# The last batch of a capacity-limited expert layer: exact rank counts against a frozen top-80 list in place of sorting, with the late weights loaded into dead attention tiles

## The chip, the cores and the metric

One core of a Trainium2 chip runs the whole program. The metric is device microseconds of one execution. Engines are named as in the profile: PE (TensorE, matmuls; PEld its weight loads), DVE (VectorE), ACT (ScalarE), POOL (GpSimd), SP (SyncE); the text uses the long names. SP issues most DMAs, POOL those of the expert weights, the gathers and the scatters.

## What is computed

Chunked sparse attention for 4 batches of 8 heads (768 tokens, 64 wide), then a mixture of 8 experts over the 3072 tokens of the attention's result (512 wide), in which each expert keeps only its 80 tokens of highest gate value:

```python
# attention, per batch and head: each query row sees its 6 best key chunks of 32 (by an upper bound), causally
scores = where(selected & causal, scale * q @ k.T, -1e9);  x = softmax(scores) @ v      # x: (3072, 512)
logits = x @ w_gate                                  # (3072, 8)
expert_idx = argmax(logits, axis=1);  gate_w = softmax(logits)[arange(N), expert_idx]
for e in range(8):
    tok_idx = where(expert_idx == e)[0]
    if len(tok_idx) > 80:
        tok_idx = tok_idx[argpartition(-gate_w[tok_idx], 80)[:80]]     # the 80 largest
    out[tok_idx] = gate_w[tok_idx, None] * (relu(x[tok_idx] @ w1[e]) @ w2[e])
```

All other rows of `out` are zero.

## The kernel before

The attention works on 8 quads of 4 heads; batch b has quads 2b and 2b+1. A quad is 6 rounds of four score steps: one round for its first 256 query rows (t = 0), two for t = 1, three for t = 2. So there are 48 rounds, numbered 0 to 47, and the loop over `rd` writes the work of all of them in one order. Inside `manual_schedule` that order is what TensorE and SyncE execute; for VectorE, ScalarE and GpSimd the scheduler fixes an order when the program is compiled, and each of these engines then executes its list strictly in that order.

One block (g, t) passes through these stages. `score` (L338) makes score matmuls, ScalarE their exponentials E (L349), and GpSimd masks the blocks on the diagonal (L352). One round later `value` (L357) and `denom` (L369) multiply E, masked, with V and with ones. After the block's last round `evacuate` (L387) copies the numerators; two rounds after it `gate_rows` (L392) adds the gate logits to the denominators and VectorE copies the result to `DSB` (L400); three rounds after it `scales` (L403) transposes DSB, takes reciprocals and, for the second quad of a batch, runs `gates` (L443), whose chain of small VectorE operations goes from `den` (L412) to `gmask` (L473): per token and expert the gate value, or -1 where the token has another expert. Four rounds after it `rows` (L427) transposes the numerators, scales them to x and stores them in `x_dram`. Meanwhile `prep` (L216) makes the next quad's K and Q (`kf`, `kmm` L235 and L237, `qp` L260), its chunk bounds (`bound`), their ranks (`rank`) and the copies of the result into QX (`unselect`, L309 and L312).

`merge` (L481) keeps the sorted 80 best gate values of each expert. TensorE transposes `gmask` to `ps_g` (8 partitions), ScalarE copies it behind the list (L487), and VectorE makes 10 MAX8 (L493) and 9 MATCH_REPLACE8 (L495) passes over 80 + 128 n values:

```python
for r in range(CAP // 8):
    nc.vector.max(out=top, in_=src[:, 0:w])
    if r < CAP // 8 - 1:
        nc.vector.match_replace(out=src[:, 0:w], in_to_replace=top, in_values=src[:, 0:w], imm_value=-2.0)
        yield
```

Batches 0 to 2 are merged at 848 wide each (the merge of batch 2 begins in round 38), batch 3 in three merges of 336 at up to four steps a round, the rest of them after the loop. Only then come the threshold `tau`, `picks`, the scan, the counts `ps_cum`, `slot`, 24 selections `sel` (L643) with 24 index matmuls (L645), and `gidx` (L651): which token sits in slot s of expert e. GpSimd gathers those rows of x with eight indirect DMAs (L656), and each expert's MLP runs (L665 and L689). The weights of experts 0 to 4 are loaded during the attention. Those of experts 5 to 7, six DMAs of 1 MB (L126, L132), go into a pool that is opened after the attention's pools are closed.

## Time and profile before

| | us |
|---|---|
| median of 3 runs (lowest, highest) | 380.48 (379.87, 381.7) |
| the profiled execution | 381.24 |
| its span, first to last instruction | 379.5 |
| mean granted TensorE clock in it | 0.902 of full speed |
| busy: PE, DVE, ACT, POOL | 291.0 (77%), 247.0 (65%), 161.8 (43%), 157.9 (42%) |

The span is what the rows below are times of: microseconds from its start. A granted clock of 1.0 is 2.4 GHz, 0.5 is 1.2 GHz. "Idle before <- releaser" in a row is how long the engine stood before it and which engine's work ended that.

### The profile page before, as it was taken

What the parts mean: (1) busy time and instruction counts of PE and PEld (TensorE: products, weight loads), DVE (VectorE), ACT (ScalarE), POOL (GpSimd) and SP (SyncE); (2) the same over time, 40 slices, a digit from 0 to 9 for tenths busy, and PEclk for the clock granted to TensorE, in tenths of its full rate; (3) what the DMA queues carried; (4) which work ended last, traced back from release to release, by engine and by line L of the source; (5) the groups of instructions that cost most, each with busy time, mean ns of one, the idle gap of its engine ahead of it and who ended that gap; (6) DMA issues with size and microseconds to landing.
All of it is one profiled execution on the core that took longest, in us unless ns stands there. A gap on an engine that the chain in (4) does not pass through costs nothing. (4 is left out here: it accounts for less than half of the span.)

```text
span 379.5 us, 9779 instructions
## 1 busy us (share of the span) xinstructions
PE 291.0 (77%) x3860; PEld 192.3 (51%) x3860; DVE 247.0 (65%) x808; ACT 161.8 (43%) x353; POOL 157.9 (42%) x360
## 2 busy tenths in 40 slices
PE   2639999999987989998978999898995303118882
PEld 1316667666644755674555667454763102116560
DVE  7684155556699856678996566799588898202331
ACT  2327548547644644764456368535550000002220
POOL 7878407816810762493047319402120050521221
PEclk9986999999999899999989999999996655557998
DMA  9972505998997499999909965000000079990110
GB/s 176 201 124 51 118 3 100 186 259 212 197 256 160 84 145 200 270 202 234 234 11 175 200 117 115 30 0 3 3 29 29 28 124 200 208 202 15 38 53 28
DMA packets 95805, 47.63 MB, mean 126 GB/s; under 512 B 76710, under 2 KB 88102, under 8 KB 95760
## 3 DMA queue, kind: packets, MB, share of 16 engines
q1 hardware_dynamic: 82320, 28.35, 34.1%
q0 software_dynamic: 13440, 18.67, 28.7%
q8 instruction: 30, 0.49, 0.6%
q14 instruction: 15, 0.12, 0.1%
HBM read 53.10 MB, written 10.76 MB: 168 GB/s over the span
## 5 line engine op out<-in xcount | busy, mean ns | idle before, releaser
L349 ACT ACTIVATE E<-ps_S 128x512 f32<-128x512 f32 x192 | 89.4, 550 | 61.1 <-PE ps_S L346 61.1
L364 PE MATMUL ps_num<-E,vn 128*32 128x256 f32 (+1 forms) x1536 | 94.2, 363 | 0.0
L352 POOL TENSOR_SCALAR_AFFINE_SELECT E<-E 128x256 f32<-128x256 f32 x96 | 37.2, 414 | 107.9 <-ACT E L349 106.7
L364 PEld LDWEIGHTS ps_num<-E,vn 128*32 128x32 f32 x1536 | 51.9, 112 | 31.6 <-issue 2.5
L383 PE MATMUL ps_den<-E,ones 128*32 128x256 f32 (+1 forms) x768 | 51.7, 359 | 4.6 <-DVE DSB L400 4.6
L493 DVE MAX8 cand<-cand 8x8 f32<-8x848 f32 (+1 forms) x60 | 45.8, 763 | 9.2 <-ACT cand L487 8.4
L346 PE MATMUL ps_S<-QX,KX 128*128 128x256 bf16 (+1 forms) x384 | 47.7, 267 | 4.3 <-ACT QX L312 2.3
L241 POOL CAST KX<-kf 64x384 bf16<-64x384 f32 x64 | 32.8, 513 | 26.8 <-ACT kf L231 24.6
L346 PEld LDWEIGHTS <-KX 128*128 128x128 bf16 x384 | 37.1, 100 | 10.5 <-issue 5.3
L495 DVE MATCH_REPLACE8 cand<-cand,cand 8x848 f32<-8x848 f32 (+1 forms) x54 | 40.4, 748 | 0.1
L383 PEld LDWEIGHTS ps_den<-E,ones 128*32 128x32 f32 x768 | 26.3, 111 | 16.5 <-DVE DSB L400 5.9
L227 PE MATMUL ps_k<-ident_f,kn 128*128 128x128 f32 x96 | 19.2, 317 | 9.4 <-DMA kn<-in_k_dram 4.8
L235 DVE TENSOR_REDUCE kmm<-kf 128x12 f32<-128x384 f32 x32 | 17.5, 546 | 12.5 <-ACT kf L231 12.2
L434 DVE TENSOR_TENSOR x_nat<-ps_xn,rec 128x512 bf16<-128x512 f32 x24 | 16.3, 680 | 10.8 <-PE ps_xn L433 10.7
L389 ACT ACTIVATE npt<-ps_num 128x512 f32<-128x512 f32 x24 | 14.3, 597 | 19.1 <-PE ps_num L364 19.1
L231 ACT ACTIVATE kf<-ps_k 128x384 f32<-128x384 f32 x32 | 16.2, 507 | 14.1 <-PE ps_k L227 8.2
L672 ACT ACTIVATE XT<-ps_XT 128x320 bf16<-128x320 bf16 x8 | 3.5, 436 | 42.2 <-PE ps_XT L669 42.2
L254 PE MATMUL ps_q<-ident_f,qn 128*128 128x128 f32 x96 | 19.0, 314 | 2.8 <-DMA qn<-in_q_dram 2.7
L682 DVE TENSOR_SCALAR HT<-ps_H 128x320 bf16<-128x320 f32 x8 | 3.9, 492 | 24.9 <-PE ps_H L679 24.9
L257 ACT ACTIVATE qf<-ps_q 128x384 f32<-128x384 f32 x32 | 16.5, 516 | 8.3 <-PE ps_q L254 8.1
L698 POOL DMA_INDIRECT out_dram<-Y,sidx x8 | 7.4, 922 | 28.2 <-DVE Y L696 25.8
L260 DVE TENSOR_SCALAR qp<-qf 128x256 f32<-128x256 f32 (+1 forms) x32 | 13.1, 411 | 8.4 <-ACT qf L257 8.4
(118 smaller groups left out, 448.5 us busy)
## 6 DMA issues: line engine op xcount, KB each, us to landing
w<-in_moe_w_dram POOLq DMA_DIRECT2D x16, 1024.0 KB, 12.7
kn<-in_k_dram SPq DMA_DIRECT2D x32, 192.0 KB, 4.0
qn<-in_q_dram SPq DMA_DIRECT2D x32, 192.0 KB, 4.7
vn<-in_v_dram SPq DMA_DIRECT2D x32, 192.0 KB, 3.7
out_dram<-zero_tile SPq DMA_DIRECT2D x12, 512.0 KB, 11.1
x_dram<-x_nat SPq DMA_DIRECT2D x12, 257.0 KB, 4.3
X<-x_dram,gidx POOLq DMA_INDIRECT x8, 6.9
out_dram<-Y,sidx POOLq DMA_INDIRECT x8, 2.6
```

Source lines behind the costliest of these rows:

```text
L227: nc.tensor.transpose(ps_k[:, j * P:(j + 1) * P], kn[:, 3 * hf + j, 2 * a:2 * a + 2, :].rearrange("p h d -> p (h d)"), ident_f32[:])
L235: nc.vector.tensor_reduce(out=kmm[a][:, 0, ch], in_=kv, axis=mybir.AxisListType.X, op=ALU.min)
L241: nc.gpsimd.tensor_copy(out=KX[s][2 * a + i][rows, cols], in_=kf[rows, :])
L254: nc.tensor.transpose(ps_q[:, j * P:(j + 1) * P], qn[:, 3 * hf + j, 2 * a:2 * a + 2, :].rearrange("p h d -> p (h d)"), ident_f32[:])
L257: nc.scalar.activation(out=qf[a][:, cols], in_=ps_q[:], func=mybir.ActivationFunctionType.Copy)
L346: nc.tensor.matmul(out=ps_S[:, r, 0:wid], lhsT=KX[s][h][:, kb * P:(kb + 1) * P], rhs=QX[s][h][:, c0:c0 + wid], start=True, stop=True)
L349: nc.scalar.activation(out=E[:, :, 0:wid], in_=ps_S[:, :, 0:wid], func=mybir.ActivationFunctionType.Exp, scale=scale)
L352: nc.gpsimd.affine_select(out=E[:, :, 0:P], in_=E[:, :, 0:P], compare_op=ALU.is_ge, fill=0.0, base=0, pattern=[[0, 2], [1, P]], channel_mu ...
L364: nc.tensor.matmul(out=NUM[q0:q0 + 32, a, c0:THIRD], lhsT=nats[(g, "vn")][:, kb, 2 * a + r, 32 * f:32 * (f + 1)], rhs=Es[st][:, r, 0:wid], ...
L383: nc.tensor.matmul(out=dn[q0:q0 + 32, c0:THIRD], lhsT=ones32[:, a, :], rhs=Es[st][:, r, 0:wid], start=first, stop=False, skip_group_check= ...
L493: nc.vector.max(out=top, in_=src[:, 0:w])
L495: nc.vector.match_replace(out=src[:, 0:w], in_to_replace=top, in_values=src[:, 0:w], imm_value=-2.0)
```

## The change

Batch 2 is no longer merged whole: its first four blocks of 128 tokens are merged at 592 wide as soon as their gates are there (rounds 35 to 38, three steps a round), its last two at 336 (rounds 38 to 41). Batch 3 is not merged at all. In round 42 the list is frozen, and `freeze` spreads over rounds 42 to 47 what stood after the loop: threshold, picks, scan, counts and slots, for the tokens of batches 0 to 2 (18 blocks instead of 24), and beside it each frozen entry's rank.

A token of batch 3 then gets its place by counting: `spread` multiplies the one-hot row of its expert (three bfloat16 parts of the gate value, so that the difference is exact) with the `lists` of the frozen values and of the new tokens, which gives all differences at once; VectorE (`own`, `count`) and ScalarE (`signs`) count how many are positive by accumulating along the row. A place below 80 is the slot that a displaced old entry leaves. Three steps, `turn_new(t)` and `weigh0` to `weigh2`, treat the three thirds of the batch, the last after the loop. The three parts of the gate come from six more operations in `gates`.

The six late weights are loaded as 18 pieces by GpSimd in rounds 40 to 44, into tiles whose last use is over (the K and Q loads, `kf`, `qf`, `qp`, the zero tile, QX and KX of the other set, the V of quad 6). GpSimd also sets up a few constants more at the start.

```diff
-    def load_w1(e, pool):
...
-    def load_w2(e, pool):
...
+    def load_parts(e, which, spaces):
...
+            tc.keep_in_program_order(nc.gpsimd.dma_start(out=dst, in_=src[:, c0:c0 + n, :]))
...
+        def late_weights(rd):
+            if rd == 40:
+                load_parts(5, 0, [bf(nats[(7, "kn")][:]), bf(zt[:])])
+            elif rd == 41:
+                load_parts(5, 1, [bf(nats[(7, "qn")][:]), bf(spare["kf0"]), bf(spare["kf1"])])
+            elif rd == 42:
+                four = [bf(spare[n]) for n in ("qf0", "qf1", "qp0", "qp1")]
+                load_parts(6, 0, [x[:, 0:DFF] for x in four])
+                load_parts(6, 1, [x[:, DFF:DFF + DMOD] for x in four])
+            elif rd == 43:
+                load_parts(7, 0, [bf(QXT[0][:])])
+                load_parts(7, 1, [bf(KXT[0][:]), bf(spare["ubS"])])
+            elif rd == 44:
+                vspace = bf(nats[(6, "vn")][:])
+                load_parts(6, 1, [vspace[:, 0:4 * DMOD]])
+                load_parts(7, 0, [vspace[:, 4 * DMOD:6 * DMOD]])
...
+        def spread(dst, c, span):
+            nc.tensor.matmul(out=dst, lhsT=lists[:, WIDE + P * c:WIDE + P * (c + 1)],
+                             rhs=lists[:, span], start=True, stop=True)
+        def own(view, c, c_lo, acc):
...
+            nc.vector.scalar_tensor_tensor(out=junk[:, 0:n], in0=view, scalar=1.0,
+                                           in1=ties[:, x0:x0 + n], op0=ALU.mult, op1=ALU.is_gt,
+                                           accum_out=acc[:, c:c + 1])
+        def signs(view, c, op, acc):
...
+            nc.scalar.activation(out=junk2[:, 0:n], in_=view, scale=2.0 ** 40,
+                                 bias=(1.0 if op is ALU.is_ge else minus1[:, 0:1]),
+                                 func=mybir.ActivationFunctionType.Sign, accum_out=acc[:, c:c + 1])
...
-            for rd in range(N + 5):
+            for rd in range(N + 1):
...
+                late_weights(rd)
...
+                if rd == FREEZE:
...
+                    fz = freeze(stages)
+                if rd >= FREEZE:
+                    next(fz, None)
+                if rd == N - 1:
+                    turn_new(0)
+                    weigh0()
...
-                    if gi == 1 and (b == NB - 1 or et == 2):
-                        n = 2 if b == NB - 1 else QBLK
-                        merges.append(merge(stages, QBLK * b + 2 * et - n + 2, n))
+                    if gi == 1 and b < NB - 2 and et == 2:
+                        merges.append(merge(stages, QBLK * b, QBLK))
+                    elif gi == 1 and b == NB - 2 and et > 0:
+                        c0, n = ((0, 4), (4, 2))[et - 1]
+                        merges.append(merge(stages, QBLK * b + c0, n))
-                if merges and rd < N:
-                    for _ in range(4 if g == NQUAD - 1 else 2):
+                if merges:
+                    for _ in range(3 if stages > 2 else 2):
...
+            last = ends[N - 1]
+            gate_rows(*last)
+            turn_new(1)
+            scales(*last)
+            weigh1()
+            rows(*last)
+            turn_new(2)
+            weigh2()
...
-        for c in range(TBLK):
-            nc.vector.tensor_scalar(out=sel[:, c, :], in0=slot1[:], scalar1=slot[:, c:c + 1],
-                                    scalar2=None, op0=ALU.is_equal)
-            nc.tensor.matmul(out=ps_idx[:].rearrange("s k e -> s (k e)"), lhsT=sel[:, c, :],
-                             rhs=slotrhs[:, c].rearrange("p k e -> p (k e)"),
-                             start=(c == 0), stop=(c == TBLK - 1))
+            nc.vector.tensor_tensor(out=sel, in0=rooms,
+                                    in1=place[:, :, None].to_broadcast([P, NEWB, CAP]),
+                                    op=ALU.is_equal)
+            for c in range(NEWB):
+                nc.tensor.matmul(out=ps_idx[:].rearrange("s k e -> s (k e)"), lhsT=sel[:, c, :],
+                                 rhs=slotrhs[:, OLDB + c, 3:5, :].rearrange("p k e -> p (k e)"),
+                                 start=(c == 0), stop=False, skip_group_check=True)
+                nc.tensor.matmul(out=ps_idx[:, 0, :], lhsT=sel[:, c, :],
+                                 rhs=slotrhs[:, OLDB + c, 5, :],
+                                 start=False, stop=(c == NEWB - 1), skip_group_check=True)
```

How it moves instructions shows on three engines. VectorE's list in rounds 36 and 37, up to the `DSB` copy of quad 5's last block, before (L309 is the last copy into QX for quad 6; `kmm` and `qp` are the K reductions and the Q copies of the next quad):

```order
L309 COPY QX_0_2_115<-ps_pen_3603 32x640
L434 TENSOR_TENSOR x_nat_2848<-ps_xn_3646,rec_3555 128x2x256
L235 TENSOR_REDUCE kmm0_3637<-kf_3657 128x12
L237 TENSOR_REDUCE kmm0_3637<-kf_3657 128x12
L235 TENSOR_REDUCE kmm0_3637<-kf_3691 128x12
L237 TENSOR_REDUCE kmm0_3637<-kf_3691 128x12
L260 TENSOR_SCALAR qp0_3641<-qf0_3639 128x256
L260 TENSOR_SCALAR qp0_3641<-qf0_3639 128x384
L235 TENSOR_REDUCE kmm1_3638<-kf_3750 128x12
L237 TENSOR_REDUCE kmm1_3638<-kf_3750 128x12
L400 COPY DSB_3800<-ps_den_189 128x256
```

The same place now, from the middle of the first merge of batch 2 (L551 is MAX8, L553 MATCH_REPLACE8; L272 to L297 are `kmm` and `qp`, L438 is the copy to `DSB`):

```order
L297 TENSOR_SCALAR qp0_3720<-qf0_3718 128x384
L553 MATCH_REPLACE cand_0_134<-cand_1_135,cand_0_134 8x592
L272 TENSOR_REDUCE kmm1_3717<-kf_3835 128x12
L551 MAX cand_1_135<-cand_0_134 8x8
L274 TENSOR_REDUCE kmm1_3717<-kf_3835 128x12
L553 MATCH_REPLACE cand_0_134<-cand_1_135,cand_0_134 8x592
L272 TENSOR_REDUCE kmm1_3717<-kf_3867 128x12
L551 MAX cand_1_135<-cand_0_134 8x8
L274 TENSOR_REDUCE kmm1_3717<-kf_3867 128x12
L553 MATCH_REPLACE cand_0_134<-cand_1_135,cand_0_134 8x592
L297 TENSOR_SCALAR qp1_3721<-qf1_3719 128x256
L438 COPY DSB_3885<-ps_den_187 128x256
```

Between the reductions now stand passes of 592, and the copy comes behind six of each kind.

ScalarE's list at the end of the attention before (`npt` are the numerators, `cand` the transposed gates for the merge, `XT` the first expert's input):

```order
L456 ACTIVATE ex_4527<-sh_4525 128x16
L487 ACTIVATE cand_0_141<-ps_g_4593 8x256
L389 ACTIVATE npt_4632<-ps_num_188 128x512
L456 ACTIVATE ex_4653<-sh_4651 128x16
L487 ACTIVATE cand_1_142<-ps_g_4692 8x256
L672 ACTIVATE XT_4865<-ps_XT_4860 128x320
```

And now (L669 copies the transposed new tokens into `lists`, L702 the rooms; L694 are the `signs`):

```order
L494 ACTIVATE ex_4843<-sh_4841 128x16
L669 ACTIVATE lists_108<-ps_n_4900 27x2x256
L702 ACTIVATE cand_1_135<-ps_rooms_4906 128x160
L694 ACTIVATE PEN_1_127,older_192<-ps_a_4914 128x80
L694 ACTIVATE PEN_1_127,older_192<-ps_a_4916 128x80
L694 ACTIVATE PEN_1_127,signed_191<-ps_a_4914 128x256
L694 ACTIVATE PEN_1_127,signed_191<-ps_a_4916 128x256
L694 ACTIVATE PEN_1_127,signed_191<-ps_l_4921,minus1_98 128x256 x2
L952 ACTIVATE XT_5013<-ps_XT_5008 128x320
```

Two copies for the merge are gone; between the last `ex` and the first `XT` stand two copies and six counts.

GpSimd's list from the end of the attention before (L126 and L132 are the late weights, L656 the gathers):

```order
L475 TENSOR_SCALAR slotrhs_140<-oh_4659,pcol_98 128x2x8
L477 TENSOR_TENSOR slotrhs_140<-oh_4659,ccol_100 128x2x8
L479 CAST slotrhs_140<-oh_4659 128x2x8
L126 DMA w1_5_4761<-in_moe_w1_dram 128x4x1024
L132 DMA w2_5_4763<-in_moe_w2_dram 128x8x512
L126 DMA w1_6_4765<-in_moe_w1_dram 128x4x1024
L132 DMA w2_6_4767<-in_moe_w2_dram 128x8x512
L126 DMA w1_7_4769<-in_moe_w1_dram 128x4x1024
L132 DMA w2_7_4771<-in_moe_w2_dram 128x8x512
L656 DMA X_4840<-x_dram_63,gidx_4838 80x257
```

The first late loads now, in rounds 40 to 42 (L150 loads a piece, named by the tile that it goes into; L390 is the mask of E):

```order
L390 AFFINE_SELECT E_4054<-E_4054 128x2x128
L390 AFFINE_SELECT E_4060<-E_4060 128x2x128
L150 DMA kn_3401<-in_moe_w1_dram 128x3x1024
L150 DMA zero_tile_110<-in_moe_w1_dram 128x1024
L150 DMA qn_3406<-in_moe_w2_dram 128x6x512
L150 DMA kf_3835<-in_moe_w2_dram 128x512
L150 DMA kf_3867<-in_moe_w2_dram 128x512
L390 AFFINE_SELECT E_4224<-E_4224 128x2x128
L390 AFFINE_SELECT E_4230<-E_4230 128x2x128
L150 DMA qf0_3718<-in_moe_w1_dram 128x1024
L150 DMA qf1_3719<-in_moe_w1_dram 128x1024
L150 DMA qp0_3720<-in_moe_w1_dram 128x1024
```

The loads stand between masks of E now, and no load stands ahead of the gathers.

## Rows read from the trace of the kernel before

**Rows 1.** Windows; us, then busy PE, PEld, DVE, ACT, POOL, clock, DMA, GB/s.

```profile
262.00:282.00 20.00, 19.79 (x310) 13.57 (x310) 14.81 (x41) 10.84 (x24) 3.73 (x11) 1.00 0.04 15
282.00:296.30 14.30, 9.74 (x111) 5.17 (x108) 11.27 (x44) 2.96 (x7) 1.43 (x5) 0.76 0.06 20
296.30:324.70 28.40, 6.47 (x36) 4.57 (x36) 25.82 (x95) 0.59 (x2) 5.67 (x9) 0.54 0.76 132
324.70:339.50 14.80, 0.05 (x2) 0.05 (x2) 0.22 (x2) 0.00 (x0) 6.72 (x8) 0.50 1.19 221
339.50:379.50 40.00, 27.99 (x352) 20.28 (x352) 9.91 (x16) 6.89 (x16) 8.02 (x9) 0.88 0.13 37
```

**Rows 2.** Timeline of the last round; start, us, engine, line, what [idle <-releaser].

```profile
282.30 1.93 PE L364 MATMUL ps_num<-E,vn 128*32 128x256 f32 x32
...
289.13 0.59 PE L486 MATMUL ps_g<-ident_f,gmask 128*8 128x128 f32 x2 [4.03 <-DVE gmask L473]
...
290.50 3.22 PE L364 MATMUL ps_num<-E,vn 128*32 128x256 f32 x32
...
295.79 0.42 DVE L400 COPY DSB<-ps_den 128x256 f32<-128x256 f32 x1 [1.77 <-PE ps_den L396]
```

**Rows 3.** Timeline from the last `DSB` to the first MLP matmul.

```profile
304.82 0.85 POOL L126 DMA_DIRECT2D w<-in_moe_w_dram  x1 [2.21 <-DVE cand L493]
...
320.58 3.69 PE L645 MATMUL ps_idx<-slotrhs,sel 128*80 128x24 bf16 x24 [2.06 <-DVE sel L643]
...
324.51 0.16 DVE L651 SCALAR_TENSOR_TENSOR gidx<-idx 80x8 int32<-80x8 f32 x1
325.57 1.03 POOL L656 DMA_INDIRECT X<-x_dram,gidx  x1 [15.72 <-issue]
...
339.24 0.90 POOL L656 DMA_INDIRECT X<-x_dram,gidx  x1 [4.21 <-DMA w<-in_moe_w_dram]
339.45 0.45 PE L669 MATMUL ps_XT<-ident_bf,X 80*128 80x80 bf16 x4 [15.19 <-DMA X<-x_dram,gidx]
...
340.50 2.29 PE L679 MATMUL ps_H<-XT,w 128*128 128x80 bf16 x32 [0.61 <-issue]
```

**Rows 4.** VectorE's groups by shape; busy us, mean ns | idle before <-releaser.

```profile
L493 DVE MAX8 cand<-cand 8x8 f32<-8x848 f32 x30 | 30.9, 1029 | 6.6 <-ACT cand L487 6.4
L495 DVE MATCH_REPLACE8 cand<-cand,cand 8x848 f32<-8x848 f32 x27 | 27.4, 1015 | 0.1
L235 DVE TENSOR_REDUCE kmm<-kf 128x12 f32<-128x384 f32 x32 | 17.5, 546 | 12.5 <-ACT kf L231 12.2
...
L493 DVE MAX8 cand<-cand 8x8 f32<-8x336 f32 x30 | 14.9, 497 | 2.6 <-ACT cand L487 2.1
...
L495 DVE MATCH_REPLACE8 cand<-cand,cand 8x336 f32<-8x336 f32 x27 | 13.0, 480 | 0.0
...
L495 DVE MATCH_VALUE_LOAD cand<-cand,cand 8x8 f32 x54 | 4.0, 74 | 0.6
```

**Rows 5.** Timeline of rounds 37 and 38: `DSB`, `gmask` and TensorE behind each.

```profile
233.52 0.42 DVE L400 COPY DSB<-ps_den 128x256 f32<-128x256 f32 x1 [0.32 <-PE ps_den L396]
...
234.42 0.39 PE L383 MATMUL ps_den<-E,ones 128*32 128x256 f32 x2
...
238.79 0.37 DVE L473 TENSOR_TENSOR gmask<-sgn,x_nat 128x16 f32<-128x16 f32 x1
...
239.75 0.60 PE L486 MATMUL ps_g<-ident_f,gmask 128*8 128x128 f32 x4
```

**Rows 6.** Timeline of round 31, where a merge of 848 runs.

```profile
204.38 0.86 PE L383 MATMUL ps_den<-E,ones 128*32 128x256 f32 x16 [1.83 <-DVE DSB L400]
```

**Rows 7.** The page's DMA issues; median us from issue to landing last.

```profile
X<-x_dram,gidx POOLq DMA_INDIRECT x8, 6.9
out_dram<-Y,sidx POOLq DMA_INDIRECT x8, 2.6
```

**Rows 8.** GpSimd's groups from 255 to 272 us; columns as in rows 4.

```profile
L352 POOL TENSOR_SCALAR_AFFINE_SELECT E<-E 128x256 f32<-128x256 f32 x10 | 3.8, 409 | 22.9 <-ACT E L349 22.9
```

More of the change, by code (lines that the diff above doesn't have):

```diff
@@ L221, in prep @@
             qp = [qfp.tile([P, SEQ], F32, name=f"qp{a}") for a in range(2)]
+            for a in range(2):
+                spare[f"qf{a}"], spare[f"qp{a}"] = qf[a][:], qp[a][:]
             def k_tile(a, hf):
@@ new lines, in gates @@
+            if new:
+                ns = slice(c0 - OLDB, c0 - OLDB + 2)
+                oh3 = entry[:, ns, 1, 0:3 * NEXP].rearrange("p c (k e) -> p c k e", e=NEXP)
+                eng = nc.vector
+            else:
+                oh3 = gsm.tile(three, BF16, name="oh3")[:]
+                eng = nc.gpsimd
+            nc.vector.tensor_tensor(out=oh3, in0=eq[:, :, None, :].to_broadcast(three),
+                                    in1=rv[:, :, None, None].to_broadcast(three), op=ALU.is_equal)
@@ L497, in merge @@
                     yield
+        idold = selp.tile([CAP, NEXP], F32, name="idold")
+        occold = selp.tile([CAP, NEXP], F32, name="occold")
+        junk, junk2 = [PEN[i][:].rearrange("p j h c -> p (j h c)") for i in range(2)]
+        counted = selp.tile([P, NEWB], F32, name="counted")
+        signed = selp.tile([P, NEWB], F32, name="signed")
+        older = selp.tile([P, NEWB], F32, name="older")
+        part = selp.tile([P, NEWB], F32, name="part")
+        halves = [x[:, 0:NEWB * CAP].bitcast(BF16).rearrange("p (w c s) -> p w c s", w=2, s=CAP)
+                  for x in cand]
@@ new lines, in cols, with turn_new @@
+        def cols(t, n=1):
+            return slice(LISTS + THIRD * t, LISTS + THIRD * (t + n))
+        def turn_new(t):
+            ps_n = misc([ROWS, 2, 2, P], BF16, "ps_n")
+            for w in range(2):
+                for j in range(2):
+                    nc.tensor.transpose(ps_n[:, w, j, :], entry[:, 2 * t + j, w, :], ident_bf[:])
+            both = lists[:, LISTS:].rearrange("k (w c) -> k w c", w=2)
+            nc.scalar.activation(out=both[:, :, THIRD * t:THIRD * (t + 1)],
+                                 in_=ps_n[:].rearrange("k w j p -> k w (j p)"),
+                                 func=mybir.ActivationFunctionType.Copy)
@@ new lines, in take_rooms, with weigh0 @@
+        def take_rooms(c0, n):
+            ps_rooms = misc([P, n, CAP], F32, "ps_rooms")
+            for j in range(n):
+                spread(ps_rooms[:, j, :], c0 + j, slice(0, CAP))
+            nc.scalar.activation(out=rooms[:, c0:c0 + n, :], in_=ps_rooms[:],
+                                 func=mybir.ActivationFunctionType.Copy)
+        def weigh0():
+            for c in (0, 1):
+                ps_a = misc([P, CAP + THIRD], F32, "ps_a")
+                spread(ps_a[:], c, slice(CAP, LISTS + THIRD))
+                count(ps_a[:, 0:CAP], c, ALU.is_ge, older)
+                own(ps_a[:, CAP:], c, 0, counted)
@@ new lines, in weigh1 @@
+        def weigh1():
+            take_rooms(0, 4)
+            for c in (2, 3):
+                ps_a = wide("ps_a")
+                spread(ps_a[:, 0:CAP + THIRD], c, slice(CAP, LISTS + THIRD))
+                count(ps_a[:, 0:CAP], c, ALU.is_ge, older)
+                signs(ps_a[:, CAP:CAP + THIRD], c, ALU.is_ge, part)
+            ps_b = wide("ps_b")
+            for c in (2, 3):
+                view = ps_b[:, THIRD * (c - 2):THIRD * (c - 1)]
+                spread(view, c, cols(1))
+            for c in (2, 3):
+                view = ps_b[:, THIRD * (c - 2):THIRD * (c - 1)]
+                own(view, c, 2, counted)
+            ps_c = wide("ps_c")
+            for c in (0, 1):
+                spread(ps_c[:, THIRD * c:THIRD * (c + 1)], c, cols(1))
+            for c in (0, 1):
+                signs(ps_c[:, THIRD * c:THIRD * (c + 1)], c, ALU.is_gt, part)
+            nc.gpsimd.tensor_scalar(out=part[:, 0:2], in0=part[:, 0:2], scalar1=0.5,
+                                    scalar2=float(P), op0=ALU.mult, op1=ALU.add)
+            nc.gpsimd.tensor_tensor(out=counted[:, 0:2], in0=counted[:, 0:2], in1=part[:, 0:2],
+                                    op=ALU.add)
+            nc.gpsimd.tensor_scalar(out=signed[:, 2:4], in0=counted[:, 2:4], scalar1=2.0,
+                                    scalar2=None, op0=ALU.mult)
+            nc.gpsimd.tensor_tensor(out=signed[:, 2:4], in0=signed[:, 2:4], in1=part[:, 2:4],
+                                    op=ALU.add)
+            nc.gpsimd.tensor_scalar(out=older[:, 0:4], in0=older[:, 0:4], scalar1=1000.0,
+                                    scalar2=48500.0, op0=ALU.mult, op1=ALU.add)
@@ L604 @@
          tc.manual_schedule(engines={mybir.EngineType.PE}):
-        class Named:
-            def __init__(self, pool, tag):
-                self.pool, self.tag = pool, tag
-            def tile(self, shape, dtype, name):
-                return self.pool.tile(shape, dtype, name=name + self.tag)
-        for e in range(NPRE, NEXP):
-            named = Named(wpc, f"_{e}")
-            weights[e] = [load_w1(e, named), load_w2(e, named)]
-        picks = selp.tile([P, 2, NEXP, TBLK], BF16, name="picks")
```

359 lines of the change are left out of this document (256 added, 103 removed).

## The prediction

> **What bounds the kernel now.** I read the windows by stage first [rows 1]. To 282 us TensorE is the bound; a window of the attention rounds shows it busy in nearly all of its time (19.79 of the 20 us from 262 to 282) at a granted clock of 1.00. Then three stretches follow in which it does little: 14.30 us for the last round, 28.40 us in which VectorE is busy for 25.82 (the last sorting passes, the threshold, the scan, the 24 selections), and 14.80 us in which no engine but GpSimd does anything and the DMA engines move weights. The 40.00 us of the expert MLP close the span. So 57.5 us lie between the last score and the first MLP matmul, and that is where the change works.
>
> The timeline says what each stretch waits for. In the last round TensorE stands 4.03 us for `gmask`, which VectorE makes between its sorting passes, and comes back at half clock: the same 32 value matmuls take 3.22 us where they took 1.93 [rows 2]. After the last `DSB` copy (its end, 296.21 [rows 2], is "D" below) the chain is VectorE's alone up to `gidx` at 324.51 + 0.16. The late weights are issued from 304.82, and the eighth gather cannot issue until 339.24, held 4.21 us by a weight; the first gather, issued at 325.57, is read by TensorE only at 339.45, and the first MLP matmul starts at 340.50 [rows 3].
>
> **The sum.** It is made against the profiled execution: 381.24 us, of which the span is 379.5. The median of the runs is 380.48, 0.76 lower.
>
> *a. Set-up.* Some ten more memsets and small operations on GpSimd ahead of the first masks, none of them above a mask's 0.41 [rows 8]: at most 4 us, of which the waits between GpSimd's first operations take most. **+0.5** (0 to 4).
>
> *b. Rounds 35 to 41.* This is the cost I believe in. Before, no sorting stands on VectorE in rounds 36 to 38. Now the first block of batch 2, 592 wide, is sorted there at three steps a round. Between the widths of 336 and 848 [rows 4] a MAX8 of 592 comes to 0.76 and a MATCH_REPLACE8 to 0.75 + 0.07 for its value load. VectorE takes its work in the order fixed at compile time, and by that order six of each now stand ahead of the `DSB` copy of quad 5's last block: 6 x 0.76 + 6 x 0.82 = 9.5 us, and with them eight reductions of K (0.55 each) and four copies that are no longer: 12 x 0.55 = 6.6. From about 227.1, when the first pass can start, that is 16.1 us: `DSB` ends at 243.2 where it ended at 233.94 [rows 5]. TensorE's next denominators stood right behind it (234.42) and wait for it: the trace has this wait already where a merge of 848 ran in the same place of a quad, 1.83 us [rows 6]. From the end of that copy to the end of `gmask` it takes 5.2 us today (233.94 to 239.16 [rows 5]); the last seven passes, 5.5 us, now stand in it, of which I let 1.9 fall into its gaps. So `gmask` of that block ends at 252.0, for which TensorE waits at the end of round 38: the place it reached at 239.75 [rows 5] it reaches 12.3 later. Of this about 0.7 comes back because one pair of transposes stands there instead of three, and 2.5 in rounds 40 to 42, where passes of 336 (0.50 and 0.48) replace passes of 848 (1.03 and 1.02) ahead of the copies into QX. **+9.0**. If TensorE's slip lets the two run beside each other the cost is 0; if nothing comes back it is 12.3, and with a like wait in the second merge 14.
>
> *c. Freezing the list, rounds 42 to 47.* New matmuls among the attention: the threshold, 720 columns of counts (0.3 at 2.4 GHz, with the wait between them 0.5), 18 index matmuls (24 took 3.69 at half clock [rows 3], so 1.4), two transposes and 640 columns for the ranks (0.4), less a pair of `ps_g` (0.3). **+2.2**, from 1 if all waits are hidden to 4 if TensorE waits once for the selections, whose 18 copies VectorE makes one after the other. VectorE itself gains time there: the 30 MAX8 and 27 MATCH_REPLACE8 of 336 of batch 3 go, and 30 and 27 of batch 2 come earlier.
>
> *d. The last round, to D.* From 282.30 (the values of the round before) to 296.21 is 13.9. The 4.03 for `gmask` goes, and with it the half clock: 1.29 for the values [rows 2], and half of that for the 16 denominators, 1.9 together: 8.0. New is the transposed list of batch 3's first third with its copy on ScalarE, behind the four E of this round (2.0 of waiting), and some 900 columns of counting (1.1): 11.1. **-2.8** (-5 to 0).
>
> *e. D to `gidx`.* Was 324.67 - 296.21 = 28.46. In its place: the 5.2 of [rows 5] for transposes and gate chain, which then had no passes between, and some six more small operations for the split of the gate value and for `entry`, half of them beside the chain (1.0): D + 6.2. Transposing it and the copy on ScalarE: D + 7.3. Then 2880 columns of spread matmuls, which I take at TensorE's lower level, 1.2 GHz, since it idles after D as today (0.54 granted in this stretch [rows 1]): D + 9.7. The counts on VectorE and the signs on ScalarE run beside them and end 1.3 later: D + 11. Place 0.6, selection in one operation 0.6, 12 index matmuls 1.2, two index operations 0.4: 13.8. **-14.7**. No row shows an operation that also accumulates along its row; the nearest are an ordinary one of the same width, and the last MAX8 passes of 336 (0.50). By the first, and with the spreads at 2.4 GHz, the end is D + 11.3; if each of some 20 on the chain costs 0.2 more, D + 18.
>
> *f. `gidx` to the first MLP matmul.* Was 340.50 - 324.67 = 15.83. The late weights are gone from the queue by then, loaded during rounds 40 to 44 into dead tiles. What is left is an issue (1.03 [rows 3]), a landing, four transposes and a copy (1.05 by 339.45 and 340.50). For the landing there is 6.9 with the weights underway, and 2.6 for transfers of the same number of rows at the end, with quiet queues [rows 7]; I take 2.6 as the nearer case: 4.7. **-11.1**, or -6.8 at a landing of 6.9.
>
> *g. MLP.* The same 352 matmuls in the same order; the cold start remains (0.88 granted [rows 1]). **0** (-2 to +2). The weights' place in memory changes no matmul.
>
> The loads themselves I cost at nothing: 18 issues by GpSimd at 0.85 to 0.93 are 15.5 us, against the 22.9 us that GpSimd waits for five masks' E from round 41 on [rows 8], and 6 MB beside a DMA share of 0.04 [rows 1]. Uncovered they would delay the masks, and with them the values.
>
> Sum: 0.5 + 9.0 + 2.2 - 2.8 - 14.7 - 11.1 = -16.9: 364.3 for such an execution, **363.5** beside the median.
>
> **The rivals.**
> *R1, no backlog.* VectorE catches up, because the reductions wait for ScalarE anyway and passes fill their gaps. For it: the reductions idle 12.5 us before they start [rows 4]. Against it: the wait of [rows 6]. Without b: 363.5 - 9.0 = 354.5.
> *R2, a long tail.* The accumulating operations are dear (+4 in e) and the gathers land as today (+4.3 in f): 372. For it: no row prices the first; against it: the transfers that slowed the gathers are gone.
> *R3, VectorE and GpSimd in each other's way.* If the 18 issues only got through while VectorE rested, each would wait for one operation of 0.55 to 0.76: 15.5 + 12 (9.9 to 13.7) = 27.5 us against 22.9 idle, 4.6 of masks late: 368. Against it: the issue at 304.82 took 0.85 [rows 3] in the stretch in which VectorE was busy for 25.82 of 28.40 us. The Trainium skill, in "SBUF — State Buffer", section "SBUF: two separate sides", calls the port pair of these two an exclusive lock and says that a transfer issued by GpSimd starves for descriptors while VectorE holds it. By that rule the time would be that of R3; this trace's 0.85 with sorting underway speaks against it.
> *R4, slower.* The early loads wait on GpSimd for their destinations: dead tiles are free only when their last reader is done, and an issue that waits holds the masks queued behind it. If issues and transfers ran in series, 15.5 + 34.4 (304.82 to 339.2, the time that six weights took) = 49.9 us less 22.9 idle: +27, 391. It decides once over 17 us beyond the idle time is exposed, for then the whole gain of 16.9 is gone. Against it: the tiles named are last read one to three rounds before.
>
> **How the numbers follow.** Forecast 0.66, R1 0.16, R2 0.11, R3 0.04, R4 0.03. The forecast's own range is 357 to 370, from the bounds of b, d, e and f, not all at once. The whole range takes in R1 and R2 with 2 or 3 us of their own: 352 to 374. A measurement of this kernel tells about 0.5% (1.9 us) from no change. Slower by that is most of R4, 0.02; no change is what is left of it and of a long tail joined to a backlog of 14, 0.02; faster 0.96.
>
> **What would show it.** Rounds 36 to 38 longer, with TensorE waiting for `DSB` and `gmask` (b); no 4 us wait in the last round (d); `gidx` some 14 us after the last `DSB` (e); the first MLP matmul under 6 us after it, with no gather held by a weight (f); GpSimd's masks no later against their E than today. A wait of TensorE for E masked by GpSimd in rounds 40 to 46 would make R3 or R4 right; a wait under 2 us in rounds 37 and 38 would make R1 right.

## The result, and the profile after

The changed kernel took 365.71 us (362.13 to 366.87, 4 runs) where the kernel before took 380.18 (378.99 to 381.7): a ratio of 0.960, 95% interval 0.953 to 0.968. It lies in the stated range, 2.2 us above the forecast. Three more sets of the same kernel gave 0.944 (0.940 to 0.948), 0.939 (0.935 to 0.943) and 0.959 (0.954 to 0.963): the kernel before repeats within about 1%, while the medians of the changed one's four sets lie on two levels, 358.5 and 360.4 us, and 365.1 and 365.7 us. Two of the four executions of the 0.939 set, at 362.2 and 362.3 us, count as slow, the profiled one among them, and stand outside that ratio. What makes the two levels is told below, with the last experiment.

The profiled execution took 366.0 us, its span is 364.1. Windows by stage, with the columns of [rows 1] (the first line is rounds 35 to 42, the second 43 to 46, then the last round to D, D to the first gather, the gathers, the MLP's last 40 us):

```profile
222.00:270.00 48.00, 39.46 (x531) 24.68 (x525) 41.86 (x133) 23.33 (x52) 27.46 (x64) 0.93 0.48 89
270.00:289.80 19.80, 19.22 (x294) 12.98 (x284) 14.81 (x71) 9.58 (x23) 7.68 (x20) 1.00 1.09 192
289.80:302.00 12.20, 10.23 (x127) 5.35 (x126) 5.56 (x28) 3.68 (x9) 1.41 (x5) 0.86 0.06 22
302.00:316.00 14.00, 5.44 (x36) 3.11 (x34) 8.13 (x43) 6.24 (x24) 2.68 (x10) 0.57 0.06 20
316.00:324.00 8.00, 3.00 (x40) 2.77 (x41) 0.49 (x1) 0.44 (x1) 5.87 (x8) 0.50 0.24 62
324.00:364.10 40.10, 25.99 (x312) 17.91 (x311) 9.42 (x15) 6.57 (x15) 8.03 (x9) 0.84 0.12 36
```

The 28.4 us of sorting after D and the 14.8 us of waiting weights are gone. VectorE, busy for 25.8 of 28.4 us in that stretch before, is now busy for 41.9 of 48 in the first line. For like rounds, 35 to 41, the same columns read, first before the change, then after it:

```profile
222.09:260.39 38.30, 35.56 (x504) 23.00 (x501) 31.29 (x97) 22.17 (x50) 15.80 (x40) 1.00 0.18 46
220.49:267.63 47.14, 38.60 (x505) 24.04 (x503) 40.96 (x134) 23.10 (x50) 25.87 (x61) 0.93 0.46 88
```

These rounds take 8.8 us longer. TensorE stands idle for 8.5 us of them instead of 2.7, and with as many matmuls it is busy 3.0 us longer, at a mean granted clock of 0.93 instead of 1.00. The timeline shows the places, first in rounds 37 and 38, to be read against [rows 5]:

```profile
239.05 0.41 DVE L438 COPY DSB<-ps_den 128x256 f32<-128x256 f32 x1
...
239.51 1.51 PE L421 MATMUL ps_den<-E,ones 128*32 128x256 f32 x16 [5.38 <-DVE DSB L438]
...
247.65 0.18 DVE L517 TENSOR_TENSOR gmask<-oh,x_nat 128x16 f32<-128x16 bf16 x1
...
247.97 0.38 PE L544 MATMUL ps_g<-ident_f,gmask 128*8 128x128 f32 x2 [1.82 <-DVE gmask L517]
```

`DSB` comes 5.5 us later than before and TensorE stands 5.38 us for it, then 1.82 more for `gmask`. Right behind the first wait it runs at half clock, and the 16 denominators take 1.51 us where they took 0.86 [rows 6]:

```profile
239.50:242.10 2.60, 2.59 (x22) 1.51 (x23) 2.50 (x6) 0.00 (x0) 0.03 (x1) 0.50 0.03 6
```

The passes have the sizes that the prediction interpolated (0.76, 0.75 and 0.50); VectorE's groups by shape:

```profile
L551 DVE MAX8 cand<-cand 8x8 f32<-8x592 f32 x10 | 7.6, 759 | 1.6 <-ACT cand L545 1.6
L553 DVE MATCH_REPLACE8 cand<-cand,cand 8x592 f32<-8x592 f32 x9 | 6.7, 747 | 0.0
L551 DVE MAX8 cand<-cand 8x8 f32<-8x336 f32 x10 | 5.0, 498 | 1.2 <-ACT cand L545 1.0
```

From the last round to the second expert the timeline reads, against [rows 2] and [rows 3]:

```profile
292.35 0.45 PE L677 MATMUL ps_a<-lists 27*128 27x336 bf16 x2 [1.66 <-ACT lists L669]
...
300.83 0.42 DVE L438 COPY DSB<-ps_den 128x256 f32<-128x256 f32 x1 [2.31 <-PE ps_den L434]
...
312.14 0.17 DVE L771 SCALAR_TENSOR_TENSOR place<-signed,counted 128x6 f32<-128x6 f32 x1 [1.19 <-ACT PEN L694]
...
314.72 0.16 DVE L792 TENSOR_TENSOR gidx<-ps_idx,left 80x8 int32<-80x8 f32 x1
...
315.17 1.05 POOL L941 DMA_INDIRECT X<-x_dram,gidx  x1 [5.05 <-DVE far L795]
...
318.93 2.29 PE L959 MATMUL ps_H<-XT,w 128*128 128x80 bf16 x32 [0.57 <-issue]
...
324.81 0.44 ACT L965 ACTIVATE HT<-ps_H 128x320 bf16<-128x320 f32 x1 [5.94 <-remote]
...
326.73 2.29 PE L959 MATMUL ps_H<-XT,w 128*128 128x80 bf16 x32 [5.25 <-ACT XT L952]
```

The wait of 4.03 in the last round has become one of 1.66 for the copy of the new tokens. D is 301.25 and `gidx` ends at 314.88: 13.63 us where it took 28.46. The first MLP matmul follows 4.05 later where it took 15.83. Then something unforeseen: ScalarE waits 5.94 us for expert 0's second half, and the second expert starts 7.8 us after the first (3.2 before). "Remote" means that the semaphore rose without an instruction's end that the profile ties to it.

By rounds (start of the first E of a round, from the timelines of ScalarE), the change's cost and gain are as follows; the 1.60 us at round 35 is not the change's, as the experiments show:

| | before | after | difference |
|---|---|---|---|
| round 35 | 222.09 | 220.49 | -1.60 |
| round 37 | 232.04 | 231.41 | -0.63 |
| round 38 | 236.04 | 242.10 | +6.06 |
| round 42 | 260.39 | 267.63 | +7.24 |
| round 47 | 281.92 | 289.79 | +7.87 |
| D | 296.21 | 301.25 | +5.04 |
| end of `gidx` | 324.67 | 314.88 | -9.79 |
| first MLP matmul | 340.50 | 318.93 | -21.57 |
| end of span | 379.5 | 364.1 | -15.4 |

### The profile page after: what moved, and what is told of

Same layout as the page of the kernel before. It is cut to its first block, busy times and chain, and to the rows that moved or that the text cites. A ratio compares the mean times of both kernels' runs of the same rounds, so it can differ in the third digit from the quotient of the medians.

```text
span 364.1 us, 9960 instructions
## 1 busy us (share of the span) xinstructions
PE 295.9 (81%) x3898; PEld 193.7 (53%) x3898; DVE 232.1 (64%) x797; ACT 168.1 (46%) x378; POOL 179.5 (49%) x435
## 5 line engine op out<-in xcount | busy, mean ns | idle before, releaser
L402 PE MATMUL ps_num<-E,vn 128*32 128x256 f32 (+1 forms) x1536 | 92.3, 357 | 0.0
L390 POOL TENSOR_SCALAR_AFFINE_SELECT E<-E 128x256 f32<-128x256 f32 x96 | 36.9, 414 | 90.5 <-ACT E L387 89.1
L402 PEld LDWEIGHTS ps_num<-E,vn 128*32 128x32 f32 x1536 | 51.1, 110 | 29.8 <-issue 1.0
L384 PE MATMUL ps_S<-QX,KX 128*128 128x256 bf16 (+1 forms) x384 | 47.7, 268 | 2.1 <-ACT QX L350 1.4
L278 POOL CAST KX<-kf 64x384 bf16<-64x384 f32 x64 | 33.1, 517 | 23.0 <-ACT kf L268 20.8
L551 DVE MAX8 cand<-cand 8x8 f32<-8x848 f32 (+2 forms) x40 | 33.1, 828 | 7.7 <-ACT cand L545 7.3
L553 DVE MATCH_REPLACE8 cand<-cand,cand 8x848 f32<-8x848 f32 (+2 forms) x36 | 29.3, 814 | 0.1
L272 DVE TENSOR_REDUCE kmm<-kf 128x12 f32<-128x384 f32 x32 | 17.4, 543 | 10.9 <-ACT kf L268 10.7
L315 PE MATMUL ps_ub<-qf,KST 128*32 128x320 f32 x128 | 15.5, 484 | 5.1 <-POOL KST L283 2.3
L471 PE MATMUL ps_xn<-ident_f,npt 128*128 128x128 f32 x96 | 15.7, 286 | 2.9 <-DVE ub L328 2.8
L263 PEld LDWEIGHTS ps_k<-ident_f,kn 128*128 128x128 f32 x96 | 12.3, 163 | 10.5 <-ACT QX L350 5.2
```

The source lines that it names most:

```text
L263: nc.tensor.transpose(ps_k[:, j * P:(j + 1) * P], kn[:, 3 * hf + j, 2 * a:2 * a + 2, :].rearrange("p h d -> p (h d)"), ident_f32[:])
L272: nc.vector.tensor_reduce(out=kmm[a][:, 0, ch], in_=kv, axis=mybir.AxisListType.X, op=ALU.min)
L278: nc.gpsimd.tensor_copy(out=KX[s][2 * a + i][rows, cols], in_=kf[rows, :])
L384: nc.tensor.matmul(out=ps_S[:, r, 0:wid], lhsT=KX[s][h][:, kb * P:(kb + 1) * P], rhs=QX[s][h][:, c0:c0 + wid], start=True, stop=True)
L390: nc.gpsimd.affine_select(out=E[:, :, 0:P], in_=E[:, :, 0:P], compare_op=ALU.is_ge, fill=0.0, base=0, pattern=[[0, 2], [1, P]], channel_mu ...
L402: nc.tensor.matmul(out=NUM[q0:q0 + 32, a, c0:THIRD], lhsT=nats[(g, "vn")][:, kb, 2 * a + r, 32 * f:32 * (f + 1)], rhs=Es[st][:, r, 0:wid], ...
```

## The experiments

The times of different chips differ by the hold-up in the MLP, so the stages of the profiles count more than the totals. All ratios are to the kernel before on the same chip. Executions also reach round 35, up to which the versions do nearly the same work, at different times (216.1 to 222.4 us). In part this is the granted clock: round 18 of the changed kernel took 4.83 us in again (first line) and 5.87 in the first profile, with the same order of instructions:

```profile
123.67:128.50 4.83, 4.83 (x72) 3.56 (x70) 4.83 (x10) 3.85 (x10) 4.24 (x12) 1.00 0.22 51
124.60:130.47 5.87, 5.87 (x74) 4.36 (x72) 5.12 (x11) 3.96 (x10) 4.61 (x13) 0.84 0.18 42
```

So the later rounds are counted from the first E of round 35 (us); added to the start of round 35 they give the time in the span, of which the expectations speak. In the changed kernel's four profiles and in rev, whose attention is the same, the time from round 35 to 47 lies between 68.4 and 69.5 us, so differences of up to 1.1 us there say nothing. A letter stands for a chip; that of the first set is not on record.

| run | chip | ratio (95%) | round 35 starts | to round 39 | to round 42 | to round 47 | first MLP matmul to end |
|---|---|---|---|---|---|---|---|
| before | | | 222.1 | 20.1 | 38.3 | 59.8 | 39.0 |
| after | | 0.960 (0.953 to 0.968) | 220.5 | 29.1 | 47.1 | 69.3 | 45.2 |
| again | A | 0.944 (0.940 to 0.948) | 220.0 | 29.2 | 46.0 | 68.4 | 38.9 |
| again2 | B | 0.939 (0.935 to 0.943) | 222.4 | 29.1 | 46.9 | 69.2 | 39.6 |
| again3 | D | 0.959 (0.954 to 0.963) | 220.6 | 29.1 | 47.1 | 69.5 | 45.1 |
| dsb_act | A | 0.935 (0.931 to 0.939) | 219.9 | 28.1 | 45.5 | 67.7 | 39.1 |
| narrow | B | 0.919 (0.915 to 0.923) | 220.7 | 20.8 | 36.4 | 59.1 | 39.5 |
| whole | A | 0.947 (0.944 to 0.950) | 220.6 | 20.0 | 44.3 | 69.5 | 39.4 |
| whole43 | B | 0.949 (0.946 to 0.952) | 220.0 | 20.0 | 44.3 | 68.7 | 39.0 |
| whole43_act | B | 0.938 (0.936 to 0.940) | 221.0 | 20.7 | 44.4 | 67.2 | 38.8 |
| lateg_act | C | 0.959 (0.955 to 0.962) | 216.1 | 22.8 | 44.6 | 72.3 | 44.7 |
| lateg_act_qp | C | 0.947 (0.945 to 0.950) | 218.3 | 20.5 | 39.2 | 65.8 | 46.2 |
| early_only | A | 0.976 (0.972 to 0.979) | 220.8 | 20.1 | 38.3 | 59.8 | 41.0 |
| rev | D | 0.966 (0.964 to 0.969) | 220.1 | 29.2 | 46.0 | 69.1 | 38.7 |

**Is it the place of `DSB`, or VectorE's load?** The prediction named the copy's place behind six passes of each kind. The first run takes the copy off VectorE:

```diff
-            nc.vector.tensor_copy(out=dsb[:], in_=dn)
+            nc.scalar.activation(out=dsb[:], in_=dn, func=mybir.ActivationFunctionType.Copy)
```

> All copies to DSB on ScalarE instead of VectorE. Theory T1 (TensorE's 5.4 us in round 37 come from the place of that copy behind six passes of each kind): the wait goes, round 38 starts 5 us sooner and at least 3 of them last to round 42; with the four smaller waits for DSB (4.4 together) the time falls by 4 to 8 us. Theory T2 (VectorE is simply full from 225 to 248, and gmask of that block cannot come sooner): the wait goes and comes back at the transposes of gmask, round 39 starts less than 1.5 us sooner, and the time falls by under 3.

Measured: round 38 starts at 235.28 (241.66 in again), round 39 at 248.06 (249.21). TensorE's longest wait from 225 to 262 us of dsb_act (in us: total, times, longest):

```profile
PE ps_g L544 <- DVE gmask L517: 6.6, 1, 6.6
```

The window of dsb_act from 225 to 250 us, with the columns of [rows 1]:

```profile
225.00:250.00 25.00, 18.17 (x228) 12.60 (x230) 23.70 (x66) 12.59 (x30) 16.00 (x37) 0.88 0.21 53
```

The wait for `DSB` went and came back whole at the next thing that VectorE owes. It is busy for 23.7 of 25 us there, and all nine MATCH_REPLACE8 of the first merge stand ahead of `gmask` in this run as in the changed kernel. So the place of `DSB` alone is not the cause: theory T2 here. The time still fell, from 0.944 to 0.935 on one chip; of the 2.5 us between the medians round 47 shows 0.8.

The second run leaves the order of the program and takes the load away. Most of batch 2 is left out of its selection; everything else is worked as before:

```diff
-            w = CAP + n * P
+            w = CAP + (n * P if stage < 2 else 16)
```

> The passes over batch 2's two merges see the list and 16 tokens only (96 wide), so most of batch 2 is left out of the selection; the same number of instructions stays. T2 (VectorE full in rounds 35 to 39 is what term b pays): with passes of some 0.15 instead of 0.5 to 0.8 us no wait of more than 1 us for DSB or gmask is left in rounds 37 and 38, round 39 starts at 240 to 242 (249.2 with the passes) and round 47 5 to 8 us sooner. Rival (the wait comes from the order, with gmask behind the passes however short): round 39 after 245.

Measured, from round 35: round 39 after 20.8 us (29.2 in again), round 47 after 59.1, 9.3 us sooner than in again and 0.8 sooner than before the change. TensorE's longest wait from 225 to 262 us:

```profile
PE ps_den L421 <- DVE DSB L438: 0.4, 1, 0.4
```

The number of instructions and TensorE's order are those of the changed kernel. VectorE's order is not: all nine MATCH_REPLACE8 of the first merge stand ahead of the copy now, where the changed kernel has six. So the rival falls all the more, and what b and c cost is the duration of the passes. Whether they cost it as load or by what stands behind them this run does not tell, since short passes make both small. The passes of batch 2 were not moved out of the tail: before, 20.1 us of them ran in rounds 38 to 43, now 24.9 run in rounds 35 to 41, since the list is frozen in round 42. What stood after D were passes of batch 3, and those are gone.

**Can it be placed better?** Fewer and wider passes, later: batch 2 merged whole, 848 wide, from round 38 (20.1 us of passes instead of 24.9).

```diff
-                    if gi == 1 and b < NB - 2 and et == 2:
+                    if gi == 1 and b < NB - 1 and et == 2:
                         merges.append(merge(stages, QBLK * b, QBLK))
...
-                    elif gi == 1 and b == NB - 2 and et > 0:
...
```

> Batch 2 merged whole again, 848 wide, from round 38 at three steps a round, in place of 592 from round 35 and 336 from round 38. T1: rounds 36 to 38 take what they took before the change (from the first E of round 36 to that of round 38 8.8 us, now 15.7), and the passes of 848 among the bounds and ranks of rounds 39 to 41 give back 2 to 4: faster by 2 to 5 us. T2 (VectorE is the bound of rounds 35 to 42 whatever the order): what rounds 36 to 38 gain comes back whole by round 42, within 1.5 us of the changed kernel.

Round 39 comes 20.0 us after round 35 as hoped (29.2 in again), but of the 9.1 us 1.7 are left at round 42, and round 43 comes 1.3 later than in again. VectorE is busy for 24.1 of the 24.2 us from round 39 to 42, and TensorE's longest wait is again for `DSB`, now in round 40:

```profile
256.16 1.92 PE L421 MATMUL ps_den<-E,ones 128*32 128x256 f32 x16 [4.20 <-DVE DSB L438]
```

T2 again: moved, not saved. But a sum over the rounds would not have told it: rounds 35 to 41 hold 36.9 us of VectorE's work here, less than the 38.3 us that they took before the change, and they take 44.3. Freezing a round later (`FREEZE = N - 5`), and then also `DSB` and the positive parts of Q on ScalarE:

> Batch 2 merged whole at 848 from round 38, and the list frozen one round later (round 43). T2: VectorE has 10 x 1.03 + 9 x 1.09 = 20.1 us of passes instead of 24.9, and TensorE no longer waits in round 42 for the end of the merge (the 2 us that round 42 to 43 took more than in the changed kernel): round 47 starts 1 to 4 us sooner than in the changed kernel. Rival: the passes of 848 now hold up rounds 41 to 43 elsewhere, round 47 within 1 us or later.

> As before, and with all copies to DSB and the positive parts of Q (qp) on ScalarE instead of VectorE, some 3.4 and 3 us less for VectorE in rounds 35 to 43. T2: another 2 to 4 us sooner at round 47 than with the later freeze alone, time near 351. Rival (ScalarE, which the exponentials need, becomes late): E of rounds 36 to 42 later, no gain.

With the later freeze round 47 comes 68.7 us after round 35, 0.3 later than in again: the rival. With 6 us of work moved to ScalarE it is 67.2, 1.5 sooner where 2 to 4 were expected, and the time ended level with the changed kernel on that chip (0.938 against 0.939). The expected 351 was missed by 6 us. From round 35 to 47 VectorE is busy for 47.7 us in whole43_act and for 47.6 in the kernel before, which needs 59.8 us for these rounds: its load alone does not set their length.

The last pair takes the wait for `gmask` out of TensorE's order: the second merge of batch 2 begins a round later.

```diff
-                    for _ in range(3 if stages > 2 else 2):
+                    for _ in range({38: 1, 39: 4, 40: 4, 41: 4}.get(rd, 3) if stages > 2 else 2):
```

> The DSB copies on ScalarE as in the run dsb_act, and the second merge of batch 2 begins in round 39 instead of 38 (one step in round 38, then four a round), so that TensorE's transposes of gmask stand a round later. In dsb_act TensorE waited 6.6 us for gmask there. If only that wait is taken away from the order: round 39 starts 5 to 6 us sooner than in dsb_act (248.1), and round 42 2 to 4 us sooner (265.4), as VectorE then still has the passes of 336 between the ranks. If VectorE's load alone counts (T2 in its strict form), the wait moves on to the ranks and the copies into QX of rounds 40 and 41, and round 42 starts within 1 us of dsb_act.

> The same, with the positive parts of Q (qp) on ScalarE too, 1.6 us a quad less for VectorE. By load alone round 42 starts another 1 to 2 us sooner than in lateg_act, and the time is 351 to 354; if ScalarE becomes late, E of rounds 36 to 41 starts later than in lateg_act and nothing is won.

From round 35, round 39 comes after 22.8 us in lateg_act, 5.3 sooner than in dsb_act, as the account by order has it. But 0.9 of that is left at round 42, and round 47 comes 4.6 us later than in dsb_act, with the same operations. VectorE is not full there, with 15.0 us busy of the 21.9 from round 39 to 42. The threshold waits for the passes that were put off, and TensorE's granted clock is low in round 39 (second line) and round 42 (third line):

```profile
264.11 0.24 PE L572 MATMUL ps_tau<-ident_f,cand 8*128 8x8 f32 x1 [1.67 <-DVE cand L551]
238.84:250.78 11.94, 9.38 (x102) 4.78 (x100) 5.24 (x25) 3.79 (x10) 5.71 (x15) 0.71 0.70 118
260.69:269.82 9.13, 6.45 (x59) 3.34 (x58) 4.79 (x12) 3.10 (x6) 4.48 (x9) 0.64 1.12 187
```

With the positive parts of Q on ScalarE too, round 42 comes after 39.2 us and round 47 after 65.8, 2.6 sooner than in again, the best of the versions that compute everything. So neither place nor load decides alone: the same operations in another order differ by 4.6 us at round 47, and the same written order with 1.6 us a quad less for VectorE by 6.4, in one profile each. Both runs stood on a chip with the hold-up in the MLP, and the time of 351 to 354 that was expected of the second was 360.8; against again3, on another such chip, lateg_act_qp has 0.947 to 0.959. The lowest ratio measured for a complete kernel is dsb_act's 0.935.

**The late weights alone.** The kernel before, with nothing but `late_weights` of the change and the pools that it needs:

```diff
-        for e in range(NPRE, NEXP):
-            named = Named(wpc, f"_{e}")
-            weights[e] = [load_w1(e, named), load_w2(e, named)]
...
+                late_weights(rd)
```

> The kernel before with nothing but its six late weights loaded in rounds 40 to 44 into the dead tiles. Theory F (the gathers of before waited for the weights, nothing else): from gidx to the first MLP matmul 4 to 5 us where it was 15.8, the attention rounds as before within 1 us, time lower by 10 to 12 (about 369) if the MLP takes 39, by 5 to 7 (about 374) if the hold-up of S1 shows here too. Rival (the early loads hold the masks of E in rounds 40 to 46): round 47 starts 2 us or more later than before.

Round 40 to round 47 took 31.0 us as before, and the time fell by 9.2 us (371.33 against 380.56). The timeline from `gidx` to the first MLP matmul:

```profile
323.34 0.16 DVE L673 SCALAR_TENSOR_TENSOR gidx<-idx 80x8 int32<-80x8 f32 x1
...
324.47 1.04 POOL L678 DMA_INDIRECT X<-x_dram,gidx  x1 [23.10 <-DVE sidx L685]
...
328.24 2.29 PE L701 MATMUL ps_H<-XT,w 128*128 128x80 bf16 x32 [0.65 <-ACT XT L694]
```

4.7 us, where it took 15.8: theory F, at the value that term f had. The time fell by a little less than the 10 to 12 us expected: the MLP took 41.0 instead of 39.0, 1.6 of the difference after the last expert's start, and that part was not followed up.

**The hold-up in the MLP.** The changed kernel was run three more times, the last time beside one that gathers in reverse order:

```diff
-        for e in range(NEXP):
+        for e in reversed(range(NEXP)):
```

> The changed kernel once more. In its first profile the first two experts of the MLP held up: ScalarE's Relu of expert 0 started 5.9 us after its input copy, where before it took 2.4, and the MLP took 45.2 us from its first matmul where before it took 39.0. Theory S1 (the gathers of experts 3 to 7, underway beside the first matmuls, hold something up): the same again here, 44 to 46 us. Theory S2 (an accident of one execution): 39 to 41 us here, and a time near 361.

> The changed kernel a third time. S2 (the hold-up of 5 us in the first two experts is an accident of single executions): the MLP takes 38.5 to 39.5 us from its first matmul, the time 356 to 362. S1 in a weaker form (it comes often): again 44 to 46 us and 365 to 367.

> The changed kernel beside the next one, on one chip. Two of the chips so far showed the hold-up in the first two experts of the MLP in their profiles (6 to 7 us: lateg_act 44.7 and lateg_act_qp 46.2 us from the first MLP matmul, the first profile of the changed kernel 45.2), two did not (38.9 to 41.0 in all their profiles). S3 (it depends on the chip): either 38.5 to 39.6 us and a time of 356 to 362, or 44 to 46.5 and 362 to 367; both are possible here.

> The gathers in reverse order, so that expert 0's rows come last and no gather is underway beside the MLP's matmuls. From gidx to the first MLP matmul some 12.5 us instead of 4.05 (seven more issues of 1.2). S1 (gathers underway beside the matmuls are needed for the hold-up): the MLP takes 38.5 to 39.6 us here even if the run beside it shows 44 or more. S4 (the chip alone): the MLP takes 44 to 46 here too if it does there. Where the run beside it shows no hold-up, this run cannot tell the two apart, and the time is about 8 us above it.

In again and again2 the MLP took 38.9 and 39.6 us, against S1 as first put, and in again3 45.1, against S2. The timeline of again3:

```profile
319.06 2.29 PE L959 MATMUL ps_H<-XT,w 128*128 128x80 bf16 x32 [0.57 <-issue]
...
323.87 0.90 POOL L941 DMA_INDIRECT X<-x_dram,gidx  x1 [0.30 <-issue]
324.89 0.44 ACT L965 ACTIVATE HT<-ps_H 128x320 bf16<-128x320 f32 x1 [5.88 <-remote]
326.30 0.44 ACT L952 ACTIVATE XT<-ps_XT 128x320 bf16<-128x320 bf16 x1 [0.97 <-remote]
```

and that of rev on the same chip:

```profile
323.12 0.90 POOL L941 DMA_INDIRECT X<-x_dram,gidx  x1 [0.30 <-issue]
...
326.71 2.29 PE L959 MATMUL ps_H<-XT,w 128*128 128x80 bf16 x32 [0.58 <-ACT XT L952]
...
329.04 0.44 ACT L965 ACTIVATE HT<-ps_H 128x320 bf16<-128x320 f32 x1 [2.38 <-PE ps_H L959]
```

Where the gathers are over before the matmuls begin, ScalarE has its input after 2.38 us (2.38 to 2.44 in all undisturbed profiles), and the MLP takes 38.7 us, beside 45.1 on that chip with seven gathers underway. rev starts its MLP 7.7 us later and ends only 1.2 later (spans 365.4 and 364.2); the medians of four executions each, 367.7 and 365.1, are 2.6 apart, where about 8 was expected if the MLPs took the same. In again, dsb_act, whole and early_only (chip A) and again2, narrow, whole43 and whole43_act (chip B) the same overlap cost at most 0.5 us, early_only's 2.0 apart. So on the one chip where it was tried the hold-up needs the gathers beside the matmuls, and something of the chip or of the hour as well. A mere accident of single executions (S2) does not fit: with the overlap it stood in all three profiles from the chips C and D, and in none of eight from A and B.

## Why the prediction was right

The time was 365.7 against 363.5, and the range held it; the sign and the mechanism of the large gains (d, e, f) held too. That it came within 2.2 us is luck: the hold-up in the MLP added 6.1 that no term had, and everything else together came out 4.6 below the forecast. By its steps, on the profiled execution (forecast -16.9, measured 364.1 - 379.5 = -15.4; 1.6 of it was there at round 35, a difference of executions):

- *a, set-up:* +0.5 forecast. Round 1 starts 1.3 us later, round 2 0.05 later: the waits took it. 0.
- *b, rounds 35 to 41:* +9.0 forecast; from round 35 to round 42 8.8 (7.7 in again). The size is right, in part by errors that cancel. `DSB` came 5.5 us later (forecast 9.3) and `gmask` 8.7 (forecast 12.8); but of the 3.2 us that were to come back by round 42 only 1.0 did. And 3.0 of the 8.8 are matmuls at a lower clock, for which b had nothing. The mechanism was half right: six passes of each kind do stand ahead of the copy, and the wait is there (5.38, forecast 8 to 9; and 1.82 for `gmask`). But the step that read the cost from the place of `DSB` fails: in dsb_act, without that place, the wait stands at `gmask`. narrow shows that the duration of the passes makes the cost, lateg_act that order among them still moves it by several us.
- *c, freezing:* +2.2 forecast; from round 42 to 47 it is 0.6 (0.8 in again). The index matmuls, priced at 1.4, took 1.22 for all 18. Batch 2 has 20 MAX8 and 18 MATCH_REPLACE8 now, not the 30 and 27 that the text of c gives. TensorE is busy 1.5 us longer in these rounds, and idle for 0.6 us of them where it was 1.5.
- *d, last round to D:* -2.8 forecast; from the E of round 47 to D it was 14.29 and is 11.46: -2.8. In again it was 9.8, with a granted clock of 1.00 in this stretch where the profiled execution had 0.85.
- *e, D to `gidx`:* -14.7 forecast, -14.8 measured (13.63 us; 13.4 to 13.7 in all runs with this tail). The end is right, its parts less so. The gate chain was 1.2 us shorter than forecast, and the counts after the spreads took longer: an accumulating operation costs an extra 0.08 us on VectorE and 0.19 on ScalarE, six of these at the end of the chain. R2 had feared 0.2 on each of some 20.
- *f, `gidx` to the first MLP matmul:* -11.1 forecast, -11.8 measured; gathers land 2.7 us after issue, as the nearer row had it. early_only shows the same by itself.
- *g, MLP:* 0 forecast, +6.1 in this execution and in again3, -0.2 to +0.5 in again and again2. 4.6 of the 6.1 stand before the second expert starts. This is the term that failed, by the hold-up that no row of before could show, since there all gathers had been issued before the MLP began [rows 3]. Without it the kernel is at 358 to 360 (again, again2), 3 to 5 us below the forecast. On the profiled execution 1.6 of these are the earlier round 35, 1.7 b and c, 0.7 f and 0.5 a.

R1 fell: round 39 starts 7.4 us late. R2 fell on both of its prices. R3 and R4 fell: GpSimd still waits for E, and no wait for a mask is among those of TensorE from 258 to 302 us. GpSimd's issues of the loads at their line in the changed kernel (nanoseconds: shortest, median, longest; then the window in us):

```profile
L150 POOL DMA_DIRECT2D qf<-in_moe_w_dram x4: 538/560/573, 264.7 to 267.3; - x4
L150 POOL DMA_DIRECT2D qp<-in_moe_w_dram x4: 551/570/588, 265.8 to 268.4; - x4
```

GpSimd's largest wait from 258 to 292 us of the changed kernel (us in total, times, longest):

```profile
POOL E L390 <- ACT E L387: 20.2, 4, 8.3
```

The 18 issues took 0.54 to 0.87 us, 11.6 together where 15.5 were assumed, in a stretch in which VectorE was busy for 41.9 of 48 us, and 20.2 us of waiting for E are left. By the rule of the Trainium skill ("SBUF — State Buffer", section "SBUF: two separate sides") GpSimd cannot write the descriptors of its DMAs while VectorE runs an operation in a two-port mode. No run here shows such a wait; which of VectorE's operations here run in that mode the trace does not tell. So the issue of 0.85 us beside the sorting, which the prediction set against R3, does not test that rule either.

## What to carry to other kernels

Work that is given an earlier due date is not free: shortening batch 2's passes gave back 9.3 us at round 47. The receiving engine's busy time, added up over the rounds in which the work must be done, is a first check, but no price: it would have passed the version whole, which won nothing. Moving the one copy that everybody waits for only showed the next wait, and putting passes off ran into the threshold. The most, 2.6 us, came back where work was taken off the engine and TensorE's order changed as well. A wait of TensorE can also cost more than its length, in matmuls at a lower clock behind it (3.0 us here). And a transfer that never overlapped a stage before is a new neighbour for it: the overlap that hid seven gathers cost at most 0.5 us in the complete kernels on two chips and 6 to 7 on others.
